# Later score steps as half-height products behind an attention output, in a fused attention and feed-forward kernel

## The chip, the cores and the metric

The kernel runs on one core of one Trainium2 chip. The metric is the device time in microseconds (us) of one execution, from the first to the last instruction with what lies around them. Five engines work side by side, each on its own list of instructions in order: PE (TensorE, matrix products), DVE (VectorE), ACT (ScalarE), POOL (GpSimd) and SP (which issues transfers here). They wait for each other by semaphores.

## The reference

```python
# q, k, v: (8, 12, 448, 64) float32; w_in: (768, 2048); w_out: (2048, 768)
scores = scale * np.matmul(q, k.transpose(0, 1, 3, 2))      # scale = 1/8
m = np.max(scores, axis=-1, keepdims=True)
e = np.exp(scores - m)
attn = e / (np.sum(e, axis=-1, keepdims=True) + np.exp(-m) + 1e-09)
x = np.matmul(attn, v)            # heads side by side: (3584, 768)
h = x @ w_in
g = h * np.tanh(log1p(exp(h)))    # mish
out = g @ w_out
```

## The kernel before, in words

Heads are worked in **pairs**: 6 pairs for each of 8 batches, 48 in all. Three pairs make a **unit** (12 score steps), so a batch is two units; units are numbered 0 to 15, and four more follow without attention. Nothing is scheduled by a tool: the order on every engine is the order in which the Python code writes the instructions, and waits are added where one instruction needs another's data or buffer.

A unit (the loop at L698) has two stretches.

The **step stretch** is a loop of 12 steps n. A pair has four score steps (s = 0 to 3): the first three treat 128 queries of both heads, the last the remaining 64 of both. Step n does, in this order:

- `exps(idx)` (L355): ACT turns score step n into exponentials, two instructions (one for s = 3), each with a sum. That frees the step's score tile. There are three score tiles in PSUM, `sc0` to `sc2`, each of two banks; step i uses tile i mod 3.
- `flush_late()` (L119): evacuations of PSUM that earlier code put off into the queue `late` are written now.
- some chunks of the **output product** g @ w_out (`mm2_part`, L565). A chunk is two products, into one of two other PSUM tiles, `mo0` and `mo1`. A portion of output columns is eight chunks and holds its tile from its first chunk until DVE has copied it out (L576). A portion of two quarters has products 384 wide and weighs 2 per chunk, a portion of one quarter 192 wide and weighs 1. `weight` (L631) says how the unit's total of 56 is spread over the 12 steps.
- `scores_ahead` (L300): the scores of step n + 3, as soon as their tile is free by the code's count. PE multiplies, and DVE takes the negated row maximum (L348), which the exponentials need.

From unit 4 on the queries stand in a block-diagonal tile `qd` with zeros, so that the scores of one head can be a product of full height, 128 rows (L329, one after the other). Where `scores_ahead` writes more than one step at once (`paired`), it uses the two products of half height (64 rows, L335 and L338), one on the upper and one on the lower rows. In the kernel before that is so only at the end of a unit, for the first three steps of the next.

The **attention output** of a pair (`av_pair`, L463: eight products, L475, exponentials times v) is made one unit later. It reads `eT`, the transposed exponentials, which a transfer on SP's queue brings (L440). From unit 4 on it stands right behind the fourth score step of a pair of the present unit, in the second bank of that step's score tile, which a fourth step leaves free; DVE casts it to `xT` (L491) at the next `flush_late`. So the three pairs' outputs come at n = 0, 4 and 8.

The **second stretch** is eight groups of six products x @ w_in (L530, `mm1_mish`), each followed by Mish on ACT (L546), in the `mo` tiles and one score tile, with the division of the exponentials on DVE (L432) and the transposing transfers beside it. At its end come the first three score steps of the next unit.

What a unit's portions are, by quarters (56 in all):

| unit | portions in order |
|---|---|
| 6, 8, 10, 12, 14 (even) | 2, 2, 2, 1 |
| 7, 9, 11, 13, 15 (odd) | 1, 2, 2, 2 |

Of the kernel before, what the change touches and what calls it, by code (L numbers as in the profile page):

```python
# [15 lines left out]
UNIT_PAIRS = 3  # L16
# [3 lines left out]
def kernel(  # L20
# [9 lines left out]
    nc = tc.nc  # L30

    B, H, S, D = q.shape
# [42 lines left out]
    mo_free = deque(mo_tiles)  # L75
# [31 lines left out]
    def divided(p):  # L107
        return p >= LATE_DIV or p in EARLY_DIV
# [7 lines left out]
    av_with, av_read, rb = {}, {}, {}  # L116
    late, held, slow = deque(), deque(), deque()

    def flush_late():  # L119
        while late:  # L120
            late.popleft()()

    def mo_take():

        if not mo_free:
            flush_late()
        return mo_free.popleft()
# [104 lines left out]
    def apart(later, *earlier):  # L232

        for e in earlier:
            tc.declare_no_dep(later.ins, e.ins, reason="they read different PSUM banks")
# [60 lines left out]
    def free_half(p):  # L296

        return sc_tiles[(p * STEPS + STEPS - 1) % len(sc_tiles)][:, 1, :]

    def scores_ahead(limit):  # L300

        n = max(0, min(limit - rg["next"], len(sc_tiles) - rg["used"]))
        for _ in range(n):
            rg["used"] += 1
            scores(rg["next"], paired=n > 1)
            rg["next"] += 1

    def scores(idx, paired=False):
# [43 lines left out]
        if s == STEPS - 1 and p in av_with:  # L352
            av_pair(av_with.pop(p), half=p)
# [106 lines left out]

        late.append(evac)

    def av_pair(p, half=None, hold=False):  # L463
        b, hp = p // HP, p % HP
        eT = att[p]["eT"]
        v_bf = casted[p]["v"]
        if b not in xT:
            xT[b] = xT_pool.tile([128, DM_T, S], BF16, tag="xT", name="xT")
        if half is not None:
            mms = av_beside.setdefault(half * STEPS + STEPS - 1, [])  # L470
        av = mo_take() if half is None else free_half(half)
        for j in range(NT):
            for h in range(2):
                e_h = eT[0:SP_, j, h * S : (h + 1) * S]
                mm = nc.tensor.matmul(  # L475
                    av[h * 64 : (h + 1) * 64, 0:S],
                    lhsT=v_bf[:, h, j * D : (j + 1) * D],
                    rhs=e_h,
                    start=(j == 0), stop=(j == NT - 1),
                )  # L480
                if half is not None:
                    apart(mm, half_max[half])
                    mms.append(mm)

        def evac():
            to = xT[b][:, hp, :]
            if p == HP:
                apart(nc.scalar.copy(to, av[:, 0:S]), half_max[half])
                return
            if divided(p):  # L490
                read = nc.vector.tensor_copy(out=to, in_=av[:, 0:S])  # L491
            else:
                read = nc.vector.tensor_tensor(
                    out=to, in0=av[:, 0:S], in1=rb.pop(p), op=ALU.mult
                )
            if half in half_exp:
                apart(read, half_exp[half])
            elif half is not None:
                av_read[half * STEPS + STEPS - 1] = read
            if half is None:  # L500
                mo_free.append(av)

        if p in spread_copy:
            late.append(spread_copy.pop(p))
        (held if hold else slow if p == HP else late).append(evac)
        del att[p], casted[p], qkT[p]

# [3 lines left out]
    def mm1_begin(b, ff, upto):  # L511

        bank = mm1_bank(ff)
        begun[b, ff] = (bank, upto)
        mm1(b, ff, bank, 0, upto)
# [90 lines left out]
    first_mm2 = 2 * UNITS_PER_B  # L606
# [22 lines left out]


    weight = [5.2] + [1.0] * (steps - STEPS) + [0.4] * (STEPS - 1)  # L631

    LEAD = UNIT_PAIRS + 1
    LOAD_AT = (0, 3, 6)
# [63 lines left out]
    for u in range(UNITS_PER_B, N_UNITS + 2 * UNITS_PER_B):  # L698
        attn = u < N_UNITS
# [2 lines left out]
            filler.extend(mm2_part(*part))  # L702
        total, done, acc = sum(w for _, w in filler), 0, 0.0
        p0 = u * UNIT_PAIRS
        if attn and u >= first_mm2:
            av_with.update({p0 + i: p0 + i - UNIT_PAIRS for i in range(UNIT_PAIRS)})
        nxt = p0 + UNIT_PAIRS
        end = min(nxt, N_PAIRS) * STEPS

        for n in range(steps):  # L710
            pi, s = divmod(n, STEPS)
            p, idx = p0 + pi, p0 * STEPS + n
            late_tp = u == UNITS_PER_B and n == STEPS
            exps(idx)
            if u == UNITS_PER_B + 1 and n == 0:
                for j in range(2):
                    turn_on_pe(HEAD, j, busy_first=3)
            flush_late()
            if late_tp:
                transpose_pair(p0 + 2)  # L720
                evac_qk(p0 + 2)
            if held and n == 1:
                late.extend(held)
                held.clear()
                flush_late()
            late.extend(slow)
            slow.clear()
            acc += weight[n]
            want = int(total * acc / sum(weight) + 1e-6)
            while done < want:  # L730
                fn, w = filler.popleft()
                fn()
                done += w
            scores_ahead(end)
            if n in LOAD_AT and u <= first_mm2:
                at = p0 + LOAD_AT.index(n)
                if u < first_mm2:
                    load_pair(at + LEAD, "qk")
                    load_pair(at + 1, "v")
                elif n == LOAD_AT[1]:  # L740
                    load_pair(nxt + UNIT_PAIRS, "qk")
                    load_pair(nxt, "v")
                cast(at + LEAD - 1, "qk")
                cast(at, "v")
            elif n == 0 and u <= N_UNITS:
                nc.gpsimd.tensor_copy(  # L746
                    out=marks[0:1, 5, 0:2], in_=att[p0 - 1]["en"][0:1, NT - 1, NTILE - 1, 0:2]
                )
                for p_ in range(p0 - UNIT_PAIRS + 1, p0 + 1):
                    if "v" in loaded.get(p_, ()):  # L750
                        cast(p_, "v")
                for i in range(UNIT_PAIRS):
                    cast(nxt + i, "kq")
                turn_by_dma(nxt)
                load_pair(nxt + UNIT_PAIRS, "kq")
                for i in range(UNIT_PAIRS):
                    load_pair(p0 + 1 + i, "v")
            if (u, n) in MORE_LOADS:
                at = MORE_LOADS[u, n]
                load_pair(at, "qk")  # L760
                load_pair(at - LEAD + 1, "v")
            if s == 0 and u > first_mm2:
                evac_qk(nxt + pi)
            if n == steps - 1 and u >= first_mm2:
                for i in range(1, UNIT_PAIRS):
                    load_pair(nxt + UNIT_PAIRS + i, "kq")
            for pe, n0 in BY_PE.items():
                j = n - n0
                first = 2 if pe == HEAD else 0
                if pe // UNIT_PAIRS == u - 1 < first_mm2 - 1 and first <= j < NT:  # L770
                    turn_on_pe(pe, j, busy_first=1)
            spread = RDEN_AT.get(u - UNITS_PER_B, {})
            if n in spread:
                on_act = u < first_mm2
                spread_rden(
                    spread[n], copy=nc.scalar.copy if on_act else nc.vector.tensor_copy,
                    behind=slow if on_act else late,
                )
            early = AV_AT.get(u - UNITS_PER_B)
            if early is not None and n in MM1_AT:  # L780
                dm = DM_T - (MM1_SHORT[MM1_AT.index(n)] if u == UNITS_PER_B else 0)
                mm1_begin(0, (u - UNITS_PER_B) * FF_U + MM1_AT.index(n), dm)
            if early is not None:
                if n in early:
                    av_pair(early[n], half=p)
            elif s == (2 if pi else 0) and N_PAIRS <= p < N_PAIRS + UNIT_PAIRS:
                av_pair(p - UNIT_PAIRS)
            if n == steps - 4 and nxt >= DIAG_FROM:
                for p_ in range(nxt, min(nxt + UNIT_PAIRS, DIAG_FROM + len(q_diag))):
                    qd = q_diag[p_ % len(q_diag)]  # L790
                    nc.gpsimd.memset(qd[0:64, S : 2 * S], 0.0)
                    nc.gpsimd.memset(qd[64:128, 0:S], 0.0)
            if u - UNITS_PER_B < len(W_AT):
                load_w(W_AT[u - UNITS_PER_B].get(n, 0))
# [7 lines left out]
        for f in range(FF_U):  # L802
# [22 lines left out]
            if f in (3, third) and p0 >= LATE_DIV:  # L825
                p = todo[1 + f // 5]
# [33 lines left out]
```

## Time and profile before

| what | value |
|---|---|
| device time, median of 3 runs (lowest to highest) | 462.04 us (460.65 to 464.67) |
| device time of the profiled execution | 460.24 us |
| its span, first to last instruction | 458.5 us |
| what lies around the span | 1.74 us |
| mean granted TensorE clock | 0.995 |
| units 6 to 15, from 142.44 to 392.97 us | 250.53 us, 25.05 each |

A row of the timeline gives the start, the time from the first start to the last end, the engine, the line, the operation with its tiles (out<-in) and shapes, and a count where equal instructions follow each other; a bracket at the end tells how long the engine had been idle and for whom it waited. The ends of products are modelled and overlap the next product, so the distance between two starts is what a product costs.

### The profile page before, as it was taken

To read this page: it belongs to the slowest core of one execution; us is meant where nothing else is said; L and a number is where in the kernel's file an instruction comes from. 1 tells how busy PE (TensorE), PEld (TensorE's weight loads), DVE (VectorE), ACT (ScalarE), POOL (GpSimd) and SP (SyncE) were. 2 spreads that over 40 slices of the span, in tenths; PEclk is the share of its full clock that TensorE was granted. 3 is DMA by queue.
4 is the path that set the end of the run, shared out by engine and by line. 5 is a ranking of instruction groups with operands and counts; after the bars stand their busy time and mean duration, and the time that the engine had idled before them with its cause. 6 is when DMAs were issued, how large, how long until landed. Compare 5 with 4: busy or idle time off the path is not lost.

```text
span 458.5 us, 8636 instructions
## 1 busy us (share of the span) xinstructions
PE 438.8 (96%) x2975; PEld 235.6 (51%) x2975; DVE 331.9 (72%) x675; ACT 330.9 (72%) x875; POOL 138.6 (30%) x269
## 2 busy tenths in 40 slices
PE   7878899999999999999999999999999999999996
PEld 3334455545545555555555554455545555556563
DVE  5999879888787978787897968897878878211021
ACT  5999788897797878787887879787878788121300
POOL 4443719043324241504324242424232300100000
PEclk9899999999999999999999999999999999999999
DMA  8999999999999999999999999999999591911122
GB/s 232 260 206 201 266 241 209 242 230 245 212 282 264 241 276 232 282 205 280 235 273 241 267 241 249 252 240 264 219 280 230 151 239 52 250 46 36 34 70 69
DMA packets 232492, 97.93 MB, mean 214 GB/s; under 512 B 189312, under 2 KB 228992, under 8 KB 232448
## 3 DMA queue, kind: packets, MB, share of 16 engines
q1 hardware_dynamic: 224928, 91.06, 85.2%
q0 software_dynamic: 7488, 6.29, 9.0%
q8 instruction: 23, 0.38, 0.3%
q14 instruction: 21, 0.17, 0.1%
q10 hardware_dynamic: 32, 0.02, 0.0%
HBM read 45.61 MB, written 11.01 MB: 124 GB/s over the span
## 4 chain that ended last, share of the span: by engine, by line
PE 70%; ACT 13%; DVE 7%; DMA 5%; issue 2%; POOL 1%; SPq 0%; DVEq 0%; ACTq 0%; POOLq 0%
PE mo L530 26%; PE mo L593 24%; ACT en L366 11%; PE sc L475 6%; DVE negm L348 5%; PE sc L329 5%; DMA eT<-en 4%; PE sc L530 4%; PE sc L335 2%; ACT L366 1%; DVE eT L455 1%; PE sc L288 1%; POOL w_in_sb L173 1%; DMA q_f<-in_q_dram 1%; PE mo L475 1%
## 5 line engine op out<-in xcount | busy, mean ns | idle before, releaser
L366 ACT ACTIVATE en<-sc,negm 128x448 bf16<-128x448 f32 x336 | 209.7, 644 | 26.7 <-DVE negm L348 25.0
L348 DVE TENSOR_REDUCE negm<-sc 128x2 f32<-128x896 f32 x192 | 179.8, 969 | 48.1 <-PE sc L338 31.6
L593 PE MATMUL mo<-w_out_sb,gT 128*128 128x384 bf16 (+1 forms) x1024 | 167.2, 307 | 0.0
L530 PE MATMUL mo<-xT,w_in_sb 128*128 128x448 bf16 x660 | 131.3, 352 | 0.6 <-DVE xT L491 0.3
L593 PEld LDWEIGHTS <-gT 128*128 128x128 bf16 x1024 | 92.5, 98 | 67.6 <-issue 18.9
L530 PEld LDWEIGHTS <-w_in_sb 128*128 128x128 bf16 x768 | 74.2, 98 | 68.8 <-issue 1.6
L546 ACT ACTIVATE gT<-mo 128x448 bf16<-128x448 f32 x110 | 58.4, 545 | 68.1 <-PE mo L530 67.9
L366 ACT ACTIVATION_READ_ACCUMULATOR en<-sc,negm 128x1 f32 x336 | 72.0, 214 | 0.0
L432 DVE TENSOR_SCALAR en<-en,rden 128x448 bf16<-128x448 bf16 x280 | 71.0, 330 | 0.6
L576 DVE COPY o_sb<-mo 128x384 f32<-128x384 f32 (+1 forms) x64 | 32.0, 499 | 48.7 <-PE mo L593 48.1
L269 POOL TENSOR_SCALAR qd<-qT_all 64x448 bf16<-64x448 bf16 x60 | 33.7, 562 | 99.8 <-DMA qT_all<-q_cast 84.6
L329 PE MATMUL sc<-kT_all,qd 128*128 128x448 bf16 x180 | 51.6, 352 | 1.4 <-ACT en L366 1.1
L475 PE MATMUL sc<-eT,v_bf 112*64 112x448 bf16 x336 | 39.8, 358 | 1.3 <-DMA eT<-en 1.3
L746 POOL COPY marks<-en 1x2 bf16<-1x2 bf16 x12 | 2.1, 176 | 98.5 <-DVE en L432 93.7
L475 PEld LDWEIGHTS <-v_bf 112*64 112x64 bf16 x384 | 18.2, 109 | 26.2 <-issue 16.5
L190 POOL CAST q_cast<-q_f 112x512 bf16<-112x512 f32 x47 | 28.7, 610 | 5.3 <-DMA q_f<-in_q_dram 5.3
L190 POOL CAST k_cast<-k_f 112x512 bf16<-112x512 f32 x47 | 28.6, 609 | 0.5 <-DMA k_f<-in_k_dram 0.5
L190 POOL CAST v_bf<-v_f 112x512 bf16<-112x512 f32 x48 | 28.1, 607 | 0.7 <-DMA v_f<-in_v_dram 0.5
L491 DVE CAST xT<-sc 128x448 bf16<-128x448 f32 x36 | 22.2, 617 | 3.3 <-PE sc L475 3.3
L335 PE MATMUL sc<-kT_all,qd 64*128 64x448 bf16 x72 | 22.0, 369 | 1.6 <-ACT en L366 1.3
L329 PEld LDWEIGHTS <-qd 128*128 128x128 bf16 x180 | 17.6, 98 | 11.1
L530 PE MATMUL sc<-xT,w_in_sb 128*128 128x448 bf16 x108 | 23.2, 353 | 0.0
(64 smaller groups left out, 254.6 us busy)
## 6 DMA issues: line engine op xcount, KB each, us to landing
k_f<-in_k_dram SPq DMA_DIRECT2D x48, 224.0 KB, 5.2
q_f<-in_q_dram SPq DMA_DIRECT2D x48, 224.0 KB, 5.1
v_f<-in_v_dram SPq DMA_DIRECT2D x48, 224.0 KB, 5.1
w_in_sb<-in_moe_w_in_dram POOLq DMA_DIRECT2D x12, 256.0 KB, 6.9
w_out_sb<-in_moe_w_out_dram POOLq DMA_DIRECT2D x8, 384.0 KB, 12.6
out_dram<-o_sb SPq DMA_DIRECT2D x7, 336.0 KB, 3.6
out_dram<-o_sb SPq DMA_DIRECT2D x8, 288.0 KB, 5.0
out_dram<-o_sb SPq DMA_DIRECT2D x8, 240.0 KB, 3.4
```

The lines of the kernel that those rows point to most:

```text
L190: nc.gpsimd.tensor_copy(out=to[nm], in_=src)
L269: q_reads.append(by.tensor_scalar(out=qd[rows, h * S : (h + 1) * S], in0=q_ps[rows, 0:S], scalar1=SCALE, scalar2=1.0, op0=ALU.mult, op1=AL ...
L329: nc.tensor.matmul(sc[:, bk, 0:S], lhsT=qT[:, 128 * c : 128 * c + 128], rhs=kT, start=True, stop=True,)
L335: nc.tensor.matmul(sc[:, 0, 0:S], lhsT=qT[0:64, qa : qa + 128], rhs=kA, start=True, stop=True)
L348: half_max[p] = nc.vector.tensor_reduce(out=negm, in_=sc[:, 0 : len(cols), 0:S], axis=AX.X, op=ALU.max, negate=True)
L366: e = nc.scalar.activation(out=st["en"][:, :, c, 0:SP_], in_=sc[:, bk, 0:S].rearrange("q (j c) -> q j c", j=NT), func=AF.Exp, bias=st["neg ...
L432: nc.vector.tensor_scalar(out=en[:, :, i, 0:SP_], in0=en[:, :, i, 0:SP_], scalar1=st["rden"][:, i : i + 1], scalar2=None, op0=ALU.mult,)
L475: mm = nc.tensor.matmul(av[h * 64 : (h + 1) * 64, 0:S], lhsT=v_bf[:, h, j * D : (j + 1) * D], rhs=e_h, start=(j == 0), stop=(j == NT - 1),)
L530: nc.tensor.matmul(bank[:, 0:S], lhsT=w_in_sb[:, dm, ff * 128 : (ff + 1) * 128], rhs=xT[b][:, dm, :], start=(dm == 0), stop=(dm == DM_T - 1),)
L546: nc.scalar.activation(out=gT[:, ff, b % 2 * S : b % 2 * S + S], in_=h_ps[:, 0:S], func=AF.Mish)
L576: nc.vector.tensor_copy(out=o_sb[:, cols.start : cols.start + n_dve], in_=st["o"][:, 0:n_dve])
L593: nc.tensor.matmul(st["o"][:, 0:n_cols], lhsT=gT[:, ff, i * 128 : (i + 1) * 128], rhs=w_out_sb[:, ff, cols], start=(ff == 0), stop=(ff == ...
```

## The change

In units 6 to 15 (`u >= PAIRED_FROM`):

- Only the first pair's attention output stays behind a fourth score step. Those of the second and third pair are written at n = 3 and n = 7 instead of 4 and 8, in an `mo` tile, and are evacuated by an ACT copy in place of DVE's cast. The copy goes into `late` and is written after the exponentials of step n + 1.
- At n = 2 and n = 6 no scores are written ahead. At n = 3 and n = 7, behind the attention output, two score steps follow at once: steps 5 and 6, and 9 and 10 (a later pair's second and third). Being two, they are products of half height.
- The chunks of the output product go by `weight_paired`: none at n = 1, 3 and 7.

With 56 spread by `weight_paired` (its sum is 52), the portions written by the end of each n are, in the weight of chunks: 18, 18, 22, 22, 26, 34, 38, 38, 44, 48, 52 (51 in an even unit), 56. In an odd unit the first portion ends at 8, the second at 24, the third at 40; in an even one at 16, 32 and 48.

```diff
-    def av_pair(p, half=None, hold=False):
+    def av_pair(p, half=None, hold=False, act=False):
...
             if p == HP:
                 apart(nc.scalar.copy(to, av[:, 0:S]), half_max[half])
                 return
+            if act:
+                nc.scalar.copy(to, av[:, 0:S])
+                mo_free.append(av)
+                return
             if divided(p):
                 read = nc.vector.tensor_copy(out=to, in_=av[:, 0:S])
...
     weight = [5.2] + [1.0] * (steps - STEPS) + [0.4] * (STEPS - 1)
+    PAIRED_FROM = first_mm2 + 2
+    AV_BEFORE = {3: 1, 7: 2}
+    weight_paired = [16, 0, 4, 0, 4, 8, 4, 0, 4, 4, 4, 4]
...
+        grouped = attn and u >= PAIRED_FROM
+        pace = weight_paired if grouped else weight
         if attn and u >= first_mm2:
-            av_with.update({p0 + i: p0 + i - UNIT_PAIRS for i in range(UNIT_PAIRS)})
+            for i in range(1 if grouped else UNIT_PAIRS):
+                av_with[p0 + i] = p0 + i - UNIT_PAIRS
...
-            acc += weight[n]
-            want = int(total * acc / sum(weight) + 1e-6)
+            acc += pace[n]
+            want = int(total * acc / sum(pace) + 1e-6)
             while done < want:
                 fn, w = filler.popleft()
                 fn()
                 done += w
-            scores_ahead(end)
+            if grouped and n in AV_BEFORE:
+                av_pair(p0 + AV_BEFORE[n] - UNIT_PAIRS, act=True)
+            if not grouped or n + 1 not in AV_BEFORE:
+                scores_ahead(end)
```

## The prediction

> **What bounds the kernel now.** I read the page's shares first, then the changed units in windows (start:end, span, busy time and instruction count of PE, PEld, DVE, ACT and POOL, granted clock, DMA share, GB/s), then one unit on PE and ACT, and last the chain that ended last.
>
> ```profile
> PE 438.8 (96%) x2975; PEld 235.6 (51%) x2975; DVE 331.9 (72%) x675; ACT 330.9 (72%) x875; POOL 138.6 (30%) x269
> ...
> 142.44:167.52 25.08, 25.01 (x158) 13.19 (x158) 20.34 (x42) 20.30 (x53) 8.88 (x18) 1.00 1.09 260
> 167.52:192.49 24.97, 24.97 (x158) 13.16 (x157) 20.04 (x42) 20.30 (x53) 8.25 (x16) 1.00 1.05 254
> 242.55:267.63 25.08, 25.01 (x159) 13.18 (x159) 20.32 (x42) 20.19 (x53) 8.89 (x18) 1.00 1.08 257
> 318.04:343.01 24.97, 24.97 (x159) 13.15 (x159) 20.04 (x42) 20.30 (x53) 8.18 (x16) 1.00 1.08 253
> sum 250.53, PE 249.89 PEld 131.81 DVE 202.90 ACT 202.55 POOL 78.23; mean PE 24.99 PEld 13.18 DVE 20.29 ACT 20.25 POOL 7.82
> ```
>
> In the ten units (142.44 to 392.97) PE is busy for 249.89 of 250.53 us at full granted clock, so PE looks like the only bound. An even unit takes 25.08 us, an odd one 24.97. Here is the even one at 242.55, PE:
>
> ```profile
> 242.55 0.36 PE L335 MATMUL sc<-kT_all,qd 64*128 64x448 bf16 x1
> 242.55 0.36 PE L338 MATMUL sc<-kT_all,qd 64*128 64x448 bf16 x1
> 242.75 0.35 PE L335 MATMUL sc<-kT_all,qd 64*128 64x448 bf16 x1
> 242.94 0.35 PE L335 MATMUL sc<-kT_all,qd 64*128 64x448 bf16 x1
> ...
> 243.22 3.42 PE L593 MATMUL mo<-w_out_sb,gT 128*128 128x384 bf16 x20
> 246.48 0.35 PE L329 MATMUL sc<-kT_all,qd 128*128 128x448 bf16 x1
> 246.76 0.95 PE L475 MATMUL sc<-eT,v_bf 112*64 112x448 bf16 x8
> 247.64 0.82 PE L593 MATMUL mo<-w_out_sb,gT 128*128 128x384 bf16 x4
> 248.31 0.54 PE L329 MATMUL sc<-kT_all,qd 128*128 128x448 bf16 x2
> 248.68 0.81 PE L593 MATMUL mo<-w_out_sb,gT 128*128 128x384 bf16 x4
> ...
> 257.62 1.00 PE L593 MATMUL mo<-w_out_sb,gT 128*128 128x192 bf16 x10
> 258.45 2.43 PE L530 MATMUL mo<-xT,w_in_sb 128*128 128x448 bf16 x12
> ```
>
> Prices by distance of starts: a wide output product (3.26/20) 0.163 us, a narrow one (0.83/10) 0.083. A score step of full height is 0.38. Its half-height form starts both products at 242.55 and gives way after 0.195; the last before other work takes 0.28, so leaving that form costs 0.09. The attention output takes 0.88 with its way out, and 0.09 more to enter (0.28 for the single product at 246.48, 0.19 without). The step stretch of this unit lasts 258.45 - 242.55 = 15.90.
>
> But a busy PE hides waits, since ends are modelled. The chain shows who releases PE in the middle of the unit:
>
> ```profile
> 248.95 1.10 DVE negm L348
> ...
> 250.08 3.82 ACT en L366 x11
> 253.90 0.04 issue
> 253.94 1.10 DVE negm L348
> ...
> 255.07 1.35 ACT en L366 x4
> 256.42 0.04 issue
> 256.46 0.35 PE sc L329
> ```
>
> From 248.95 to 256.42 the chain runs over DVE and ACT, and ends in a score step of PE that waited for a free tile. PE and the loop score, maximum, exponential, free tile are nearly even.
>
> ```profile
> 244.57 0.63 ACT L366 ACTIVATE en<-sc,negm 128x448 bf16<-128x448 f32 x1
> 245.10 0.19 ACT L366 ACTIVATION_READ_ACCUMULATOR en<-sc,negm 128x1 f32 x1
> 245.19 0.62 ACT L366 ACTIVATE en<-sc,negm 128x448 bf16<-128x448 f32 x1
> ...
> 250.08 0.64 ACT L366 ACTIVATE en<-sc,negm 128x448 bf16<-128x448 f32 x1 [1.09 <-DVE negm L348]
> ...
> 255.07 0.63 ACT L366 ACTIVATE en<-sc,negm 128x448 bf16<-128x448 f32 x1 [0.56 <-DVE negm L348]
> ```
>
> An exponential takes 0.61 to the next, and its tile is free 0.72 after its start (245.10 + 0.19). The maximum that ACT awaits at 250.08 starts 0.45 after the step's second product (248.31 + 0.19) and ACT starts 1.13 later. ACT idles 1.09 and 0.56 in the unit.
>
> **The change, part by part.** *Half height.* Four steps per unit go from 0.38 each to 0.195 + 0.28 for two. The way in is the attention output's own way out: at 45.88 a half-height step follows 0.88 after an attention output's start, as the output product does at 247.64.
>
> ```profile
> 45.00 0.95 PE L475 MATMUL sc<-eT,v_bf 112*64 112x448 bf16 x8
> 45.88 0.36 PE L335 MATMUL sc<-kT_all,qd 64*128 64x448 bf16 x1
> ```
>
> So a unit saves 2 x (0.76 - 0.475) = 0.57, ten units 5.7. The number of products stays; the entry of 0.09 moves from the fourth score step to the chunk ahead.
>
> *Copy for cast.* DVE loses 20 casts, off the path. ACT gains 20 copies; the same shape from PSUM is here once, and two Mish from PSUM follow each other closely:
>
> ```profile
> L488 ACT CAST xT<-sc 128x448 bf16<-128x448 f32 x1 | 0.5, 527 | 0.0
> ...
> 261.13 0.98 ACT L546 ACTIVATE gT<-mo 128x448 bf16<-128x448 f32 x2
> ```
>
> I take 0.53 to the end and 0.44 (0.98 - 0.54) to the next instruction; bounds 0.44 and the exponential's 0.64. Two per unit fit into ACT's idle 1.65. What counts is what waits for them: the `mo` tile. An output portion needs the other tile when it starts, and there the attention output now sits, until a copy that stands behind the exponentials of steps 4 and 8.
>
> *Even unit*, time from its first score product: half-height steps to 0.67; 18 wide 3.60; step 3 and output 4.76; step 4 5.14; 4 wide and entry 5.88; output 6.76; steps 5 and 6 7.24; 4 wide 7.89; step 7 needs tile 1. Step 4's second product began at 4.95, its maximum 5.40, exponentials 6.53 and 7.14, free at 7.86 + 0.04 = 7.90: no wait. Step 7 to 8.09, 8 wide to 9.39. The third portion starts at 9.07, the copy is done by 6.53 + 1.22 + 0.53 = 8.28: no wait. Step 8 needs step 5's tile: 6.76 + 0.45 + 1.13 + 0.61 + 0.72 + 0.04 = 9.71, a wait of 0.3. Then step 8 to 10.09, 4 wide and entry 10.83, output 11.71, steps 9 and 10 12.19, 6 wide 13.17, step 11 13.36, 4 wide 14.01, 16 narrow 15.34. Against 15.90: **-0.56**.
>
> *Odd unit*: 16 narrow and 10 wide to 3.63, alike to 7.27, 2 wide to 7.60, and now, at weight 24, the third portion starts. Step 4: second product 4.98, maximum 5.43, exponentials 6.56 to 7.78, copy to 8.31, PE goes on at 8.35: a wait of 0.75. Then 2 wide, step 7, 8 wide, step 8 (second product at 10.37), 4 wide and entry, output, steps 9 and 10, 2 wide: 12.97, and the fourth portion starts at weight 40. Step 8's maximum 10.82, exponentials 11.95 to 13.17, copy to 13.70: a wait of 0.77. From 13.74: 4 wide, step 11, 12 wide: 16.53. Before, the odd unit at 167.52 went over to L530 here:
>
> ```profile
> 183.27 0.92 PE L530 MATMUL mo<-xT,w_in_sb 128*128 128x448 bf16 x4
> ```
>
> 15.75 after its start. So an odd unit **loses 0.78**. The second stretch is unchanged: ACT ends step 11 at 16.5 (even) and 17.0 (odd), about as in the unit shown (256.42 and behind it a last exponential), and Mish comes in time.
>
> *Transfers.* None is added, and none changes its place in SP's or POOL's queue. But the second pair's output comes at 5.9 instead of 9.2 and the third's at 10.8 instead of 14.2, so `eT` and the cast v must be there sooner. v is (here 0.05 after the unit's start):
>
> ```profile
> 240.89 1.71 POOL L190 CAST v_bf<-v_f 112x512 bf16<-112x512 f32 x3
> ...
> 143.99 3.75 SPq L440 DMA_TRANSPOSE eT<-en  x1
> ...
> DMA to landing us min/median/max: 5.2/5.2/5.2
> ...
> 316.88 3.64 SPq L440 DMA_TRANSPOSE eT<-en  x1
> ...
> DMA to landing us min/median/max: 6.9/6.9/6.9
> ```
>
> The second transfer for the unit at 142.44 lands at 149.2, 6.8 after its start: PE waits 0.9, and the exponentials behind it move along. For the unit at 318.04 it lands 5.8 after, just in time. I take 0.9 once; zero is the lower bound, 0.9 in each of five even units and 0.3 in each odd one the upper (there the tile is awaited anyway, and only step 8's exponentials start later: 6.8 + 0.88 + 0.45 + 1.13 + five at 0.61 = 12.3 against 11.95).
>
> *Sum*: 5 x (-0.56) + 5 x 0.78 + 0.9 = +2.0. The profiled execution took 460.24 (span 458.5 and 1.74 around it), hence 462.2; the median of the runs is 1.8 above it, so 462.04 + 2.0 = **464.0**.
>
> **Rivals.** *The tile comes in time.* If the copy ran ahead of the exponentials, its output done at about 7.1 and copied by 7.6, the odd units would gain as the even ones: 10 x -0.56 = -5.6, 456.4 by the median. For it speaks that ACT idles 1.09 just there; against it that the copy is written behind both exponentials of step 4. The Trainium skill, PSUM — Partial Sum Buffer, Engine vs sequencer instructions, says that ScalarE's queue is strictly first in, first out, so by it this rival falls; ACT's rows here stand in program order, and no run shows one that overtook.
>
> *The transposed exponentials come late (slower).* Place: the second pair's output at 5.9. It decides once the second transfer lands later than that. If all ten land as the one at 142.44, the upper bound above holds: 5 x 0.9 + 5 x 0.3 - 0.9 = +5.1 on the forecast, 469.1. For it: landings are 1.5 apart in the rows shown, with DMA shares over 1.0; against it: the other lands at 5.8.
>
> *No gain from half height.* If the won 0.57 is only waited away on the loop of DVE and ACT, every unit gives it back: 464.0 + 5.7 = 469.7. For it speaks the chain; against it that steps 4 and 8 come a microsecond sooner (5.14 against 6.13), which pulls the loop along. The Trainium skill, TensorEngine Tiling (Array Packing), PSUM Bottleneck, says that tiling speeds up the products but not the evacuation of PSUM; by that rule this rival is the outcome, by the rows only step 8's wait of 0.3 agrees. If the halves didn't overlap at all behind an output (that the change does not do what it says), the price would be like it; the two starts at 242.55 speak against it.
>
> **How the numbers follow.** Forecast 0.55, tile in time 0.15, late transfers 0.2, no gain 0.1. About 1% (4.6 us) is what a measurement of this kernel can tell from no change. The forecast's own range, 460.5 to 467.5, is mostly inside it; 0.08 of it lies above. The first rival lies mostly below -1%, the last two nearly all above +1%. Faster 0.12, within 1% 0.53, slower 0.35. The range is 458.0 to 469.5, which leaves out most of the first rival and the end of the last.
>
> **What would show it.** Right: even and odd units apart, about 24.5 and 25.8 us; in odd ones gaps of PE near 7.6 and 13.0 before an L597 product (the output product's new line), ended by ACT's copy; two half-height starts 0.195 apart behind each later output; ACT's idle before step 4 gone into the copy. Wrong: odd units as short as even ones, PE waiting for `eT` in most units, or even units no shorter than 25.

## The result, and the profile after

The changed kernel takes 464.78 us (median of 22 runs, 461.69 to 469.47) against 461.82 for the kernel before on the same chip (22 runs, 459.05 to 468.04). The ratio is 1.0065, with a 95% interval of 1.0041 to 1.0089: slower by a little over half a per cent. The profiled execution took 464.4 us, with a span of 462.6.

The shares of the page:

```profile
PE 433.5 (94%) x2975; PEld 230.1 (50%) x2975; DVE 320.0 (69%) x655; ACT 340.9 (74%) x895; POOL 138.2 (30%) x269
```

The units 6 to 8 in windows, and the sum over all ten (columns as in the prediction):

```profile
143.79:169.81 26.02, 24.45 (x159) 12.68 (x159) 19.17 (x40) 21.31 (x55) 8.67 (x18) 1.00 1.10 260
169.81:195.55 25.74, 24.54 (x158) 12.58 (x157) 19.07 (x40) 21.21 (x55) 9.15 (x18) 1.00 1.11 252
195.55:220.14 24.59, 24.41 (x160) 12.60 (x159) 19.16 (x40) 21.20 (x55) 7.94 (x16) 1.00 1.02 241
...
sum 253.34, PE 244.77 PEld 126.18 DVE 191.22 ACT 212.53 POOL 77.87; mean PE 24.48 PEld 12.62 DVE 19.12 ACT 21.25 POOL 7.79
```

PE's busy time falls by 5.1 us in the ten units (244.77 against 249.89), near the 5.7 that the products were to save, and yet the ten units together become 2.8 longer (253.34 against 250.53). What PE saves, it waits away, and more. It does so in every second unit: 24.6 in units 8, 10, 12 and 14, 25.7 in odd ones, 26.0 in unit 6. (Unit 11 took 26.11, but it stood out before too: 25.32 where the prediction has 24.97 for an odd unit.) The span grew by 4.1; the other 1.35 lies ahead of unit 6 (it starts at 143.79 instead of 142.44), where the code is the same. The edits have moved the lines behind them: the output product is L597 here, x @ w_in L534 and its Mish L550. (Of two experiments, narrow_last and from_unit_7, the profiled execution had a lower mean clock, 0.983 and 0.981, so only units at a granted clock of 1.00 are read from them.)

PE's waits from 140 to 400 us (engine, tile and line <- releaser: us in total, times, longest):

```profile
PE mo L597 <- ACT xT L491: 6.3, 10, 1.0
PE sc L329 <- ACT en L366: 1.3, 5, 0.6
PE mo L475 <- DMA eT<-en: 1.0, 1, 1.0
```

Before, there was one wait of 0.3 in this stretch. Now the output product waits ten times, twice in each of the five odd units, for ACT's copy; an even unit waits once for an exponential to free a score tile; and one attention output waits for a transfer. These are three of the prediction's places. Here is the odd unit that starts at 169.81, first PE around its waits:

```profile
176.61 0.36 PE L335 MATMUL sc<-kT_all,qd 64*128 64x448 bf16 x1
...
176.81 0.35 PE L335 MATMUL sc<-kT_all,qd 64*128 64x448 bf16 x1
...
177.09 0.50 PE L597 MATMUL mo<-w_out_sb,gT 128*128 128x384 bf16 x2
...
178.19 0.48 PE L597 MATMUL mo<-w_out_sb,gT 128*128 128x384 bf16 x2 [0.60 <-ACT xT L491]
...
183.59 0.65 PE L597 MATMUL mo<-w_out_sb,gT 128*128 128x384 bf16 x3 [0.60 <-ACT xT L491]
```

ACT around the first of them:

```profile
176.38 0.63 ACT L366 ACTIVATE en<-sc,negm 128x448 bf16<-128x448 f32 x1 [0.20 <-DVE negm L348]
...
177.01 0.62 ACT L366 ACTIVATE en<-sc,negm 128x448 bf16<-128x448 f32 x1
...
177.62 0.53 ACT L491 CAST xT<-mo 128x448 bf16<-128x448 f32 x1
```

The half-height steps stand behind the output 0.20 apart. Two products of the next portion go into its tile at 177.09; the third portion then needs the other tile, in which the attention output lies. ACT works on both exponentials of step 4 first, copies from 177.62 to 178.15, and 0.04 later PE goes on. Two products cost 0.33, so PE could have gone on at 177.42: the wait is 0.77. The bracket says 0.60, because the modelled end of a product runs into the idle time. At 183.59 the same happens at step 8.

### The profile page after: what moved, and what is told of

It reads as the page before. It is cut to its first block, busy times and chain, and to the rows that moved or that the text cites. A ratio compares the mean times of both kernels' runs of the same rounds, so it can differ in the third digit from the quotient of the medians.

```text
span 462.6 us, 8655 instructions
## 1 busy us (share of the span) xinstructions
PE 433.5 (94%) x2975; PEld 230.1 (50%) x2975; DVE 320.0 (69%) x655; ACT 340.9 (74%) x895; POOL 138.2 (30%) x269
## 4 chain that ended last, share of the span: by engine, by line
PE 66%; ACT 10%; DMA 9%; DVE 7%; issue 4%; POOL 2%; SPq 0%; DVEq 0%; POOLq 0%
PE mo L597 25%; PE mo L534 24%; DMA eT<-en 9%; ACT en L366 8%; DVE negm L348 5%; PE sc L534 4%; PE sc L475 3%; PE sc L329 3%; PE sc L335 3%; PE mo L475 3%; POOL w_in_sb L173 1%; ACT xT L491 1%; PE sc L288 1%; DVE xT L495 1%; DVE eT L455 1%
## 5 line engine op out<-in xcount | busy, mean ns | idle before, releaser
L597 PE MATMUL mo<-w_out_sb,gT 128*128 128x384 bf16 (+1 forms) x1024 | 163.8, 307 | 6.3 <-ACT xT L491 6.3
L534 PE MATMUL mo<-xT,w_in_sb 128*128 128x448 bf16 x660 | 131.3, 353 | 0.6 <-DVE xT L495 0.3
L597 PEld LDWEIGHTS <-gT 128*128 128x128 bf16 x1024 | 93.0, 98 | 71.5 <-issue 24.1
L550 ACT ACTIVATE gT<-mo 128x448 bf16<-128x448 f32 x110 | 58.8, 544 | 69.0 <-PE mo L534 68.5
L534 PEld LDWEIGHTS <-w_in_sb 128*128 128x128 bf16 x768 | 74.2, 98 | 68.6 <-issue 1.6
L335 PE MATMUL sc<-kT_all,qd 64*128 64x448 bf16 x112 | 32.9, 363 | 1.6 <-ACT en L366 1.3
L338 PE MATMUL sc<-kT_all,qd 64*128 64x448 bf16 x112 | 33.0, 364 | 0.0
L329 PE MATMUL sc<-kT_all,qd 128*128 128x448 bf16 x100 | 30.1, 353 | 2.1 <-ACT en L366 2.1
L475 PE MATMUL mo<-eT,v_bf 112*64 112x448 bf16 x208 | 24.6, 358 | 1.1 <-DMA eT<-en 1.0
L534 PE MATMUL sc<-xT,w_in_sb 128*128 128x448 bf16 x108 | 23.2, 353 | 0.0
L475 PE MATMUL sc<-eT,v_bf 112*64 112x448 bf16 x176 | 20.8, 358 | 2.3 <-DMA eT<-en 2.3
```

What stands on the lines that cost most here:

```text
L329: nc.tensor.matmul(sc[:, bk, 0:S], lhsT=qT[:, 128 * c : 128 * c + 128], rhs=kT, start=True, stop=True,)
L335: nc.tensor.matmul(sc[:, 0, 0:S], lhsT=qT[0:64, qa : qa + 128], rhs=kA, start=True, stop=True)
L338: nc.tensor.matmul(sc[:, 1, 0:S], lhsT=qT[64:128, qb : qb + 128], rhs=kB, start=True, stop=True)
L475: mm = nc.tensor.matmul(av[h * 64 : (h + 1) * 64, 0:S], lhsT=v_bf[:, h, j * D : (j + 1) * D], rhs=e_h, start=(j == 0), stop=(j == NT - 1),)
L534: nc.tensor.matmul(bank[:, 0:S], lhsT=w_in_sb[:, dm, ff * 128 : (ff + 1) * 128], rhs=xT[b][:, dm, :], start=(dm == 0), stop=(dm == DM_T - 1),)
L550: nc.scalar.activation(out=gT[:, ff, b % 2 * S : b % 2 * S + S], in_=h_ps[:, 0:S], func=AF.Mish)
```

## The experiments

Each ratio is to the kernel before on the same chip, with its 95% interval; it is worked out over the runs and need not be the quotient of the medians. Edits are against the changed kernel, but for the last. The stronger evidence is the length of the units, which repeats within 0.05 us between profiles where nothing late is involved, while whole executions vary by more than 1%. Unit 11 is an exception: it is 0.35 longer than the other odd units in the kernel before, the changed kernel, full_height and before_stores_behind, and not so in the others. Why stays open.

**Even units alone.**

```diff
-        grouped = attn and u >= PAIRED_FROM
+        grouped = attn and u >= PAIRED_FROM and u % 2 == 0
```

> The change in units 6, 8, 10, 12 and 14 alone; the odd ones as before. Tile theory (the loss sits in odd units, where an output portion starts while its tile still holds an attention output that waits for ACT's copy): the even units stay at 24.6 us but for unit 6 (26.0, its transposed exponentials are late), the odd ones go back to 25.0; 4 x -0.50 + 0.94 = -1.1 us against the kernel before, ratio 0.998. Rival (copies on ACT and earlier transfers cost every unit alike): about half of the whole loss stays, +1.5 us, ratio 1.003.

Measured: 459.65 us, ratio 0.9995 (0.9958 to 1.0031). The even unit at 192.34 (the odd ones keep their 24.97):

```profile
192.34:216.92 24.58, 24.40 (x158) 12.60 (x158) 19.53 (x40) 21.23 (x55) 8.43 (x17) 1.00 1.05 248
```

The ten units take 249.2, 1.3 less than before, near the expected 1.1, and no L597 product waits. That the sums agree is partly chance: units 6 and 14 each waited 0.5 for a transposed pair (unit 14, at 25.17, gained nothing), and unit 11 lacked the 0.35 that it had before. The ratio alone, with 1.3 us at stake, tells nothing; the units do.

**Odd units alone.** The same line with `u % 2 == 1`.

> The change in units 7, 9, 11, 13 and 15 alone; the even ones as before. Tile theory: odd units at 25.75 us, even ones at 25.1, 5 x 0.78 = +3.9 us against the kernel before, ratio 1.008, more than the whole change loses. Rival (every unit alike): +1.5 us, ratio 1.003.

Measured: 466.24 us, ratio 1.0101 (1.0065 to 1.0136). An odd and an even unit:

```profile
170.51:196.27 25.76, 24.55 (x159) 12.60 (x159) 19.79 (x40) 21.25 (x55) 8.65 (x18) 1.00 1.08 250
196.27:221.35 25.08, 25.01 (x158) 13.18 (x158) 20.33 (x42) 20.19 (x53) 8.80 (x17) 1.00 1.02 248
```

PE's waits from 140 to 400 us:

```profile
PE mo L597 <- ACT xT L491: 6.1, 10, 0.6
```

The loss sits in the odd units, and the ten waits for the copy are the only ones there. The ten units take 254.09, 3.6 more than before (expected 3.9). In this profile the attention part ahead of unit 6 was slow as well: unit 4, with the same code in all these kernels, took 29.4.

**Portions of an odd unit as 2, 2, 2, 1** (narrow_last), which moves the bounds of the portions to those of an even unit, for groups 0 to 2:

```diff
-            plan[u0 + 1] = [(g, 1, 1, 1), (g, 1, 2, 2)] + whole(g, 2)
+            narrow = [(g, 1, 1, 1)]
+            plan[u0 + 1] = [(g, 1, 2, 2)] + whole(g, 2) + narrow if g < 3 else narrow + [(g, 1, 2, 2)] + whole(g, 2)
...
-        plan[u0 + 3] = [(g, 4, 3, 1)] + whole(g, 5) + [(g, 6, 0, 2)]
+        narrow = [(g, 4, 3, 1)]
+        plan[u0 + 3] = whole(g, 5) + [(g, 6, 0, 2)] + narrow if g < 3 else narrow + whole(g, 5) + [(g, 6, 0, 2)]
```

> The changed kernel, with the narrow portion of the odd units written last instead of first, so that portions start at weights 16, 32 and 48 in all units and none right behind an attention output. The same products. Tile theory: the two PE gaps of 0.77 us go, odd units drop from 25.75 to 24.6 us; 9 units at -0.4 to -0.5 and unit 6 at +0.94 give -3.1 us against the kernel before, ratio 0.993. Rival (the copies or the loop over maxima and exponentials hold the odd units): they stay at 25.4 or more, ratio 1.005.

Measured: 460.69 us, ratio 0.997 (0.9939 to 1.0). Units 7 (on time) and 9 (late):

```profile
172.24:196.83 24.59, 24.41 (x160) 12.60 (x159) 19.16 (x40) 21.23 (x55) 8.62 (x17) 1.00 1.02 262
221.41:246.46 25.05, 24.45 (x158) 12.68 (x158) 19.16 (x40) 21.22 (x55) 8.54 (x17) 1.00 1.07 237
```

PE's waits from 140 to 400 us:

```profile
PE sc L329 <- ACT en L366: 2.2, 10, 0.6
PE mo L475 <- DMA eT<-en: 1.7, 3, 0.9
PE mo L475 <- DVE negm L348: 1.2, 2, 0.6
```

The mechanism holds: the ten waits for the copy are gone, and odd units reach 24.58. The size is missed: of 3.1 us only 1.1 came (the ten units take 249.47). In five of them the second pair's output now waits 0.4 to 0.9 us by the brackets; where the profile names DVE, that maximum was long done and the transfer landed just then. What was one late transfer in the changed kernel is now the next bound.

**The change from unit 7 on** (`PAIRED_FROM = first_mm2 + 3`), which leaves unit 6 its old order.

> The changed kernel, begun one unit later, so that unit 6 stays as before. Late-transfer theory (unit 6 alone pays, its second transposed pair lands 6.8 to 7 us after its start): unit 6 goes from 26.0 back to 25.1, -0.9 us against the changed kernel, +2.0 against the one before, ratio 1.0045. Rival (it is the first changed unit that pays, whatever its transfers): unit 7 then pays 0.9 on top of 25.75, and the ratio stays at 1.0065 or goes to 1.008.

Measured: 464.67 us, ratio 1.0066 (1.0034 to 1.0097), so the ratio doesn't tell this kernel from the changed one. The units 6 and 7:

```profile
150.00:175.58 25.58, 25.08 (x158) 13.33 (x158) 20.66 (x42) 20.30 (x53) 8.76 (x17) 1.00 1.10 256
175.58:201.33 25.75, 24.54 (x158) 12.59 (x157) 20.00 (x40) 21.25 (x55) 8.44 (x17) 1.00 1.08 258
```

Unit 6 is 0.44 shorter than with the change (26.02) and unit 7 pays nothing in its place; the ten units take 252.56. So the cost of the late second transfer does not pass on to the next unit. Unit 6 is still not at the 25.08 of the first profile. Its wait is another one here:

```profile
PE sc L475 <- DMA eT<-en: 0.4, 1, 0.4
```

It stands at the first pair's output (in a score tile, 4.7 us after the unit's start), whose transfer landed just then. In the changed kernel's unit 6 that output did not wait.

**Steps 5, 6, 9 and 10 at full height again**, everything else as changed.

```diff
-            scores(rg["next"], paired=n > 1)
+            scores(rg["next"], paired=n > 1 and not whole)
...
-                scores_ahead(end)
+                scores_ahead(end, whole=grouped)
```

> The changed kernel with steps 5, 6, 9 and 10 as products of full height again; places, copies and portions as changed. 0.57 us more of products per unit. Loop theory (in odd units the half-height gain is waited away, since PE stands at the tile that is free at 8.35 us whether it comes at 7.6 or 7.9): odd units stay at 25.75, even ones go from 24.6 to 25.1; 5 x 0.5 = +2.5 us on the changed kernel, ratio to the one before 1.012. Rival (each unit pays what its products cost): odd units 26.3, even ones 25.15, +5.7 us, ratio 1.019.

Measured: 467.44 us, ratio 1.0151 (1.0112 to 1.019). An even and an odd unit:

```profile
194.78:219.82 25.04, 24.93 (x159) 13.16 (x159) 19.17 (x40) 21.23 (x55) 8.03 (x16) 1.00 1.03 247
219.82:245.58 25.76, 25.09 (x159) 13.15 (x159) 19.09 (x40) 21.27 (x55) 8.97 (x18) 1.00 1.08 248
```

PE's waits from 140 to 400 us:

```profile
PE mo L597 <- ACT xT L491: 3.7, 10, 0.7
```

In both units half height saves PE 0.5 us of products. In the even one that shortens the unit by 0.46 (25.04 to 24.58). In the odd one it is worth nothing (25.76 against 25.75): full height only makes PE arrive later at the same tile, and the waits shrink from 6.3 to 3.7 in all.

**Half height alone**: the outputs go back behind the pairs' fourth steps, in the score tile, with DVE's cast; the half-height steps and `weight_paired` stay.

```diff
-            for i in range(1 if grouped else UNIT_PAIRS):
+            for i in range(UNIT_PAIRS):
...
-            if grouped and n in AV_BEFORE:
-                av_pair(p0 + AV_BEFORE[n] - UNIT_PAIRS, act=True)
```

> The other part alone: steps 5, 6, 9 and 10 in half height and the portions by the new weights, but all attention outputs at their old place behind the fourth score step, with DVE's cast. By the products a unit would save 0.57 less two entries of 0.09, 0.39 us: 24.6 to 24.7 us, ratio 0.991. Loop theory: without the 0.88 us of attention output ahead of them PE comes to steps 6, 7 and 11 before their tiles are free (6.1 against 6.45, 7.4 against 7.9, 13.0 against 13.5) and waits 1.4 us; all units, even and odd, at 25.8 us, +7.5 us, ratio 1.016.

Measured: 470.02 us, ratio 1.0193 (1.0165 to 1.0222). A unit:

```profile
193.03:218.93 25.90, 24.93 (x158) 12.53 (x158) 20.32 (x42) 20.20 (x53) 8.99 (x18) 1.00 1.02 242
```

PE's waits from 140 to 400 us:

```profile
PE sc L329 <- ACT en L366: 7.7, 20, 0.5
PE sc L335 <- ACT en L366: 1.8, 8, 0.2
```

Two steps written at once want two free score tiles, and the second (step 6) waits for its own. The larger waits are at the single steps 7 and 11 behind the pairs: by the distances of starts 0.4 at step 6, 0.5 at step 7 and 0.6 at step 11 in the unit shown. PE comes there before the tiles are free. Each unit loses 0.8 to 0.9. The early output is therefore part of the gain in even units. It doesn't pull step 4 forward (that starts 4.8 after the unit's start here and in the changed kernel alike, by the new portions); it gives PE 0.88 us of products while the tiles come free. Neither part alone gains: the early output without half height leaves even units at 25.04, against 25.08 before.

**The copy ahead of the exponentials**, written at once and not through `late`.

```diff
-        (held if hold else slow if p == HP else late).append(evac)
+        if act:
+            evac()
+        else:
+            (held if hold else slow if p == HP else late).append(evac)
```

> The changed kernel with ACT's copy written ahead of the exponentials of steps 4 and 8 instead of behind them. Tile theory alone: the tile is free at 7.6 us, odd units drop to 24.6, ratio 0.993. Loop theory: ACT now waits for the attention output (until 7.0) before step 4's exponentials, which start at 7.45 instead of 6.56, and step 7's tile is free at 8.85 instead of 7.9; the wait only moves to the score steps, and even and odd units come alike, at 25.4 us; about +4 to +5 us against the kernel before, ratio 1.010.

Measured: 466.21 us, ratio 1.0146 (1.0109 to 1.0183). An even and an odd unit:

```profile
193.35:218.82 25.47, 24.54 (x159) 12.59 (x159) 19.26 (x40) 21.02 (x55) 8.80 (x17) 1.00 1.01 252
218.82:244.34 25.52, 24.54 (x158) 12.59 (x157) 19.17 (x40) 21.03 (x55) 8.51 (x17) 1.00 1.10 249
```

PE's waits from 140 to 400 us:

```profile
PE sc L329 <- ACT en L366: 9.5, 20, 0.7
...
```

The copy on ACT in the even unit:

```profile
200.24 0.53 ACT L491 CAST xT<-mo 128x448 bf16<-128x448 f32 x1 [0.46 <-PE mo L475]
```

The wait for `mo` goes, and twenty waits for a score tile take its place, two per unit: ACT stands 0.46 for the attention output with exponentials queued behind the copy. Odd units gain 0.23 by it, even ones lose 0.89. The place behind the exponentials is the better one of the two. (One transposed pair was late there as well, by 1.4, in unit 6.)

**The cast on DVE**, at the same place in `late`.

```diff
-                nc.scalar.copy(to, av[:, 0:S])
+                nc.vector.tensor_copy(out=to, in_=av[:, 0:S])
```

> The changed kernel with DVE's cast in place of ACT's copy, written at the same place in the code. On DVE that place lies behind the maxima of steps 5 and 6 (7.2 to 9.3 us), so the tile is free at 9.95 us instead of 8.35. Tile theory: odd units wait 2.3 us and more at each of two portions and the loop behind it slips too, 28 to 29 us; even ones wait about 0.9 at the third portion, 25.8 us; 15 to 22 us more than the kernel before. Rival (DVE has room, 20 us busy of 25): no more than the changed kernel, 25.75 and 24.6.

Measured, one run: 485.96 us. An odd unit:

```profile
170.82:199.69 28.87, 24.54 (x158) 12.60 (x159) 20.32 (x42) 20.63 (x53) 8.38 (x17) 1.00 0.94 226
```

PE's waits from 140 to 400 us:

```profile
PE mo L597 <- DVE xT L491: 26.5, 19, 2.2
...
```

DVE in the odd unit:

```profile
178.10 2.09 DVE L348 TENSOR_REDUCE negm<-sc 128x2 f32<-128x896 f32 x2 [0.73 <-PE sc L338]
180.10 0.61 DVE L491 CAST xT<-mo 128x448 bf16<-128x448 f32 x1
```

Even units take 25.90, where 25.8 was expected. PE's products are the same as in the changed kernel, 24.54 busy. The cast stands behind the maxima of steps 5 and 6, two microseconds, and PE waits as long. Neither copy nor cast is dear by itself (0.53 and 0.61): the place in the queue is.

**Without the stores of groups 0 to 2**, on top of narrow_last. This kernel leaves out part of the output, so its time is read for the waits alone.

```diff
-            elif have + nq == 4:
+            elif have + nq == 4 and g == B // 2 - 1:
```

> The kernel with the narrow portion last, which leaves out the stores of the finished output rows in units 6 to 15 (three of four groups; 1.3 MB of about 6.3 MB that a unit moves), so its time is not that of the whole work. With the narrow portion last, units 9, 10, 12 and 13 waited 0.5 to 0.7 us for transposed exponentials before the second attention output. If the load on the transfer engines and SP's queue makes them late, the second transfer now lands earlier than 5.9 us into the unit and these units go to 24.6 us; unit 6 too, or nearly. If the lateness comes from when the division on DVE ends (no stores would change that), units keep their waits of 0.5 to 0.7.

Measured, one run: 453.99 us. Unit 9, which was late in narrow_last:

```profile
214.84:239.41 24.57, 24.39 (x158) 12.59 (x157) 19.15 (x40) 21.20 (x55) 8.51 (x17) 1.00 1.03 226
```

PE's waits from 140 to 400 us:

```profile
PE sc L329 <- ACT en L366: 2.2, 10, 0.6
...
```

All ten units but the first (24.96) come down to 24.6 or less and nothing waits for `eT`. The second transfer lands 3.2 to 4.9 us after its unit's start, against 6.2 to 6.7 in the waiting units of narrow_last. So the transfers were late through the stores, and not because the division ahead of them was late; whether through the stores' load or their place in SP's queue this run can't tell. The second transfer isn't the slow one: it lands 5.2 to 6.9 after its issue in the waiting units, and 5.0 to 6.8 without the stores. But it is issued behind the unit's first one, and that holds the queue for 4.3 to 6.4 us in the waiting units, against 3.4 to 4.6 without the stores. (In narrow_last's units 11 and 12 a first transfer of 5.1 and 5.3 was still in time.) (The expectation names unit 12; the waiting units of narrow_last are 6, 9, 10, 13 and 14.)

**A version that beats both: narrow_last from unit 7 on**, with the copy given more room at n = 5.

```diff
-    PAIRED_FROM = first_mm2 + 2
+    PAIRED_FROM = first_mm2 + 3
...
-    weight_paired = [16, 0, 4, 0, 4, 8, 4, 0, 4, 4, 4, 4]
+    weight_paired = [16, 0, 4, 0, 4, 10, 2, 0, 4, 4, 4, 4]
```

> The narrow portion last, begun at unit 7, and two of the output product's weight moved from n = 6 to n = 5 (the wait of 0.34 us at step 8 is then filled with products). By the products and the tile a changed unit takes 24.25 to 24.35 us; if no transfer is late, nine units at -0.7 give -6.5 us against the kernel before, ratio 0.986. If transfers are late as in the kernel with the narrow portion last (0.5 to 0.7 us in about half of the units, more often as units get shorter), it is -3 to -4 us, ratio 0.993. I expect the second.

Measured: 458.58 us against 460.01, ratio 0.9899 (0.9834 to 0.9963). Units 7 and 8:

```profile
167.79:192.07 24.28, 24.28 (x159) 12.69 (x159) 20.28 (x40) 21.09 (x55) 7.20 (x15) 1.00 1.10 247
192.07:218.22 26.15, 24.39 (x158) 12.76 (x157) 19.68 (x40) 21.34 (x55) 9.25 (x18) 1.00 1.06 254
```

PE's waits from 140 to 400 us:

```profile
PE mo L475 <- DMA eT<-en: 4.1, 5, 1.2
PE mo L475 <- DVE negm L348: 0.6, 1, 0.6
```

Faster than both kernels (the changed one by its ratio of 1.0065 on another chip), though by how much is not settled: the medians are 0.3% apart, and the ratio rests on few runs, of which two, at 453.75 and 454.12, pull it down. Where nothing is late, a unit takes 24.28 and PE is busy in all of it. Unit 8 takes 1.9 more, for transfers alone. The ten units take 248.6 in this profile, 2.0 less than before, where 3 to 4 was expected.

**Its stores written later on SP's queue**, behind the unit's three transposing transfers (stores_behind; a list holds them until then), and, as a control, **the same in the kernel before** (before_stores_behind).

> The kernel with the narrow portion last, begun at unit 7, with the stores of finished output rows (three of four groups) written on SP's queue behind the unit's three transposing transfers instead of ahead of them. The same bytes. If it is the stores just ahead in the queue that make the transposed exponentials late (without the stores every second transfer landed at 3.2 to 4.9 us), the second transfers land by 5.9, changed units take 24.3 us, and the ratio to the kernel before goes from 0.990 to about 0.985. If it is the whole load on the transfer engines, only their order in the queue changes: units keep waits of 0.6 to 1.2 us in half of the cases, ratio 0.990, and the loads behind the stores come later.

> The kernel before with the stores moved in the same way, as a control. There the second attention output comes at 9.2 us and the second transfer lands at 6.8 at the latest, so an earlier landing is worth nothing in the ten units: ratio 0.997 to 1.003. Rival (the earlier transfers help by themselves): 0.99.

Measured: 458.65 us, ratio 0.9948 (0.9906 to 0.999), and for the control 463.44, ratio 1.0025 (0.9987 to 1.0064). PE's waits in the first (the attention output is L476 there):

```profile
PE mo L476 <- DVE negm L349: 1.2, 2, 0.6
PE mo L476 <- DMA eT<-en: 1.1, 2, 1.0
PE sc L476 <- DMA eT<-en: 0.5, 1, 0.5
```

Waits for `eT` are fewer in this profile (2.8 us in all against 4.7), and the ten units are shorter (246.7 against 248.6). But second transfers still land up to 7.3 after the unit's start, and the ratio is not better: its interval overlaps that of the version above. So the order on SP's queue isn't shown to be the cause; the control is unchanged within its interval. What stays open is which of the loads and stores slow a transposing transfer, and whether spreading them would bring all units to 24.28.

## Why the prediction was right, point by point

- **Even unit, -0.56.** Measured -0.50 in units 8, 10, 12 and 14, with the wait at step 8 that was worked out as 0.3:

```profile
205.33 0.54 PE L329 MATMUL sc<-kT_all,qd 128*128 128x448 bf16 x2 [0.18 <-ACT en L366]
...
210.96 1.30 PE L534 MATMUL mo<-xT,w_in_sb 128*128 128x448 bf16 x6
```

By the distance of starts it is 0.34 (again more than the bracket), and the step stretch ends 210.96 - 195.55 = 15.41 after the unit's start (15.34 was worked out).

- **Odd unit, +0.78.** Measured +0.77 to +0.79, each against the same unit before (25.32 to 26.11 for unit 11). PE goes on after the two tile waits 8.38 (178.19 - 169.81) and 13.78 after the unit's start; 8.35 and 13.74 were worked out. The waits are 0.77 and 0.77, against 0.75 and 0.77.
- **Late transfer once, 0.9.** Right in its place, with some luck, and too small in its price. The prediction looked at two of the ten second transfers. In the same trace the one for unit 9, issued at 217.5, landed 6.4 later and 6.3 after its unit's start, also later than 5.9; in the changed kernel it landed at 5.86, just in time. The transfer for unit 6 lands about 7 us after the unit's start:

```profile
150.77 0.95 PE L475 MATMUL mo<-eT,v_bf 112*64 112x448 bf16 x8 [1.01 <-DMA eT<-en]
```

Against another even unit, unit 6 lost 26.02 - 24.58 = 1.44. The wait itself is 1.01; the other 0.4 is the wait at step 8, which grows from 0.34 to 0.72. The prediction noted that the exponentials behind move along, but put no price on it. In unit 6 the change cost 0.94 where the sum had -0.56 + 0.9 = +0.34.
- **The sum, +2.0.** The ten units became 2.8 longer: 4 x (-0.50) + 5 x 0.78 + 0.94. Of the 0.8 beyond the sum, unit 6 makes 0.6 and the four other even units 0.2. The profiled execution grew by 4.2, of which 1.35 lies ahead of the change. The medians on one chip are 3.0 apart. The forecast of 464.0 rests on a median of 462.04 before; here that was 461.82, so part of the nearness to 464.78 is luck of some tenths.
- **The tile comes in time.** It falls as said: in even units the tile is free in time, in odd ones it is not. The two rows of ACT at 177.01 and 177.62 show the copy behind both exponentials. The Trainium skill, PSUM — Partial Sum Buffer, Engine vs sequencer instructions, has ScalarE's queue as strictly first in, first out; copy_first agrees, for there step 4's exponentials began at 200.67, behind a copy that waited 0.46, though their maximum was done at 199.87. But the conclusion "copied early, all units gain" was wrong: early copying moved the wait and both units took 25.5. What lets all units gain is where the consumer takes the tile (narrow_last).
- **No gain from half height.** Half right, by unit: 0.46 earned in even units, nothing in odd ones (full_height), and a loss where the outputs are not early (half_height_alone). So the rival's price, 5.7 for ten units, was too high: the odd units' +0.78 had the saving waited away already, and only 5 x 0.46 = 2.3 was left to lose. The Trainium skill, TensorEngine Tiling (Array Packing), PSUM Bottleneck, holds that tiling speeds up products and not the evacuation. The odd units agree: 0.5 us less of products, and no less time, since PE waits there for an evacuation. In even units PE doesn't wait for it, and the saving counts.
- **The transposed exponentials come late.** In the changed kernel only unit 6 waited. It decides as soon as the tile wait is gone: in narrow_last, and in the version from unit 7 on. That the longer odd units gave the transfers the time they needed is argued, not shown. For it speaks that in even_only, with odd units of 24.97, unit 14 was late as well.

## What to carry to other kernels

Where PE and another engine's loop are nearly even, price a saving of PE at the next wait behind it: write down, per unit, when the tile, the maximum and the transfer are there, and when PE comes for each. An evacuation that is cheap by itself can cost more than it lasts by what stands ahead of it in its engine's queue, and moving the point at which the consumer takes the tile may cure that where moving the evacuation doesn't. A unit made shorter may leave its transfers too little time (in narrow_last, four units that had been in time were late), so look in the profile for transfers that land with little to spare before removing the wait ahead of them.

## What was not expected of the hardware

The spread of the transposing transfers. On SP's queue, 140 to 400 us, first the kernel before (duration min/median/max in ns, then us from issue to landing):

```profile
L440 SPq DMA_TRANSPOSE eT<-en x33: 3477/3692/5532, 139.2 to 395.1; - x33
...
DMA to landing us min/median/max: 5.0/5.4/8.2
```

Then narrow_last:

```profile
L440 SPq DMA_TRANSPOSE eT<-en x33: 3462/3643/6411, 142.5 to 397.7; - x33
...
DMA to landing us min/median/max: 5.0/5.4/8.7
```

Without the stores:

```profile
L440 SPq DMA_TRANSPOSE eT<-en x32: 3406/3538/4597, 139.9 to 388.7; - x32
...
DMA to landing us min/median/max: 5.0/5.1/6.8
```

Equal transfers hold their queue for 3.5 to 6.4 us and land 5.0 to 8.7 after issue; without the stores the longest landing is 6.8. Most of this tail stands in the profile of the kernel before (landings up to 8.2); the prediction's two rows, 5.2 and 6.9, don't show it. Code that no edit touched varied too: unit 4 took 26.0 us before, 27.3 after and 29.4 in odd_only, in the latter with waits of PE for transfers (3.5 us in all from 85 to 140 us, against 1.3 before).
